# A written-out order of tasks and PSUM banks in place of a list scheduler, in a gated spectral and dense mix

## The chip, the cores and the metric

The kernel runs on one core of a Trainium2 chip. The metric is the device time of one execution in microseconds, as a median over runs. The engines are TensorE (PE, with its weight loads as PEld), VectorE (DVE), ScalarE (ACT), GpSimd (POOL) and SyncE (SP). Each runs its own instruction stream in order, and the streams meet at semaphores. SP, ACT and POOL also issue DMAs, which run on 16 engines that all queues share.

## The reference: what is computed

```python
x = A_x                                             # (1, 2048, 512) bf16
g = sigmoid((x * gate_w).sum(-1, keepdims=True))    # one gate a row
X = rfft2(x, axes=(-2, -1)) * (w_r + 1j * w_i)      # w: (2048, 257)
a = irfft2(X, s=(2048, 512))                        # spectral branch
h = x @ w1 + b1                                     # (2048, 512) @ (512, 1792)
b = (h * tanh(softplus(h))) @ w2                    # mish, (1792, 512)
return g * a + (1 - g) * b
```

There are two branches over the same 2048 x 512 input. The dense branch is two matrix products with a Mish between them. The spectral branch is a two-dimensional real Fourier transform, a product with a weight per frequency, and the way back; the kernel does the transforms as products with constant matrices. A gate per row mixes the two.

## The kernel before, in words

The program is a graph of 578 tasks, each with an engine, its reads and writes, and a few instructions. A task's name tells its stage:

- `ld_x`, `ld_w1`, `ld_w2`, `ld_W` and others are loads. x comes in pieces: x0 to x3 one row tile each, x4 and x6 two tiles (256 KB), x8 and x12 four tiles (512 KB). SP and ACT issue x, w1 and the constants at the start. POOL issues the two halves of w2 (`ld_w2_0`, `ld_w2_1`, 896 KB each) and the eight pieces of the spectral weight (`ld_W00` to `ld_W13`, 257 KB each), all behind the landing of `ld_sm`.
- `warm` and `tr` are the first TensorE work: 16 matmuls on zeros, and transposes of x (line 525), four for a row tile. `tr_small` transposes the bias. `evx` evicts them into xT. `table` (line 470) is a Mish of one element, ahead of which ScalarE loads its function table.
- Dense: `mm1_c_ft` (line 846) is four 128x512 matmuls for chunk c of 512 rows (0 to 3) and feature tile ft (0 to 13); `mish_c_ft` (line 853) evicts it on ScalarE with Mish into one of three buffers. `mm2_t_0` and `mm2_t_1` (line 870) are the two halves of the second product for row tile t, seven matmuls each; the first half reads `ld_w2_0`, the second `ld_w2_1`. Row tile 15 is cut by columns instead. `bev_t` evicts a row tile with the factor (1 - g), `sum_t` adds the spectral part, `out` stores it; tiles 14 and 15 use `fin_t` (line 882), which does both in one instruction.
- Spectral forward: `a10_t` and `a11_t` (line 563, four matmuls each) transform two row tiles along the row, `eg`, `e1p`, `e1m`, `e1f` evict and combine them, `s1_t` (line 594, 16 matmuls) is the first step along the columns, `e2_t` evicts it into Ybuf, and `r1w` stores it to a scratch tensor in DRAM in 16 pieces. When all 16 have landed `r1r0` to `r1r3` read it back in another layout into Abuf. `s2_vc` (line 735) is the second step, `wm` multiplies by the weights on VectorE, `wz` combines on GpSimd, `s2i_v` (line 766) starts the way back. `s2c`, `cvec`, `crv`, `rcc` and others handle one column apart; `wcols` on GpSimd and `rcw` on TensorE (lines 640 and 641) prepare its weights and need all eight `ld_W`.
- Spectral back: `e4`, `r2w`, `r2r` are a second trip through DRAM, into T2r; then for each of 16 row tiles `s1i` (line 795), `e5`, `a1i` (line 807), `gc`, `sap` and `sam` (line 818), `sbp` and `sbm` give the spectral part in `ga`.
- `gdot`, `gpow`, `gadd`, `gcol`, `omg` make the gates.

PSUM has eight banks. A task that starts a product names the banks it may have, and whoever gets a bank next waits for all readers of what stood there.

What sets the order of the work is `_Graph.schedule`, a list scheduler that runs when the program is built. It keeps a modelled time per engine, takes the ready tasks whose modelled start is within 0.03 us of the earliest, and picks the one with the highest priority (a table `PR` by stage, with a little random noise from a fixed seed), then the longest remaining path. It picks the engine for tasks that can run on several, and the bank that is free first. The result is one list of tasks per engine; semaphore waits are derived from it. `run_engine` then emits each list. At the end of SP's list stand the closing waits:

```python
for t in G.tasks:
    if t.isdma and t.sem is not out_sem and seen.get(t.sem.num, 0) < t.semval:
        eobj.wait_ge(t.sem, t.semval)
eobj.wait_ge(out_sem, 16 * n_out_dma[0])
```

They ask for every DMA that SP hasn't waited for already; there are 38 of these (the loads, ld_g1, ld_gd and the four r2r). In the program they stand two to an instruction.

Of the kernel before, what the change touches and what calls it, by code (L numbers as in the profile page):

```python
# [107 lines left out]
class _Ps:  # L108


    __slots__ = ("options", "bank", "sl", "nfree", "consumers", "done")

    def __init__(self, options):
        self.options = [o if isinstance(o, tuple) else (o,) for o in options]
        self.bank = None
        self.nfree = 0
        self.consumers = []
        self.done = 0.0
# [30 lines left out]
SCH = dict(eps=0.03, sync=0.05)  # L149
LAT = {"act": 0.11, "dve": 0.08, "pool": 0.05, "pe": 0.0, "sp": 0.0}  # L150


class _Graph:
# [49 lines left out]
    def schedule(self):  # L203
        tasks = self.tasks
        sync = SCH["sync"]
        eps = SCH["eps"]
        for t in tasks:
            for d in t.deps:
                d.succ.append(t)
        for t in reversed(tasks):  # L210
            m = 0.0
            for s_ in t.succ:
                m = max(m, s_.bl)
            t.bl = t.dur + t.lat + t.xfer + m
        nleft = {id(t): len(t.deps) for t in tasks}
        ready = [t for t in tasks if not t.deps]
        rng = np.random.RandomState(SEED)
        prio = {id(t): t.prio + OFFS.get(_kind(t.name), 0.0) + NOISE * rng.uniform(-1, 1) for t in tasks}
        free = {e: 0.0 for e in self.ENGS}
        order = {e: [] for e in self.ENGS}  # L220
        bank_free = [0.0] * 8
        bank_prev = [()] * 8
        port = 0.0
        dq = 0.0
        gen = {}
        left = len(tasks)
        while left:
            cand = []
            for t in ready:
                opts = t.opts or ((t.eng, t.dur, t.fn, t.lock),)  # L230
                bo = None
                for (oe, od, of, ol) in opts:
                    e_ = max(free[oe], port) if ol else free[oe]
                    for d in t.deps:
                        e_ = max(e_, d.start + d.dur if d.eng == oe == "pe" else d.done + (0.0 if d.eng == oe else sync))
                    if oe == "pe" and e_ < COLD:
                        od *= 2
                    if bo is None or e_ + od < bo[0] - 1e-9:
                        bo = (e_ + od, e_, oe, od, of, ol)
                est = bo[1]  # L240
                if t.alloc is not None:
                    got, used = [], set()
                    for p in t.alloc:
                        best = None
                        for o in p.options:
                            if any(bank_free[b] is None or b in used for b in o):
                                continue
                            f = max(bank_free[b] for b in o)
                            if best is None or f < best[0] - 1e-9:
                                best = (f, o)  # L250
                        if best is None:
                            break
                        est = max(est, best[0] + sync)
                        got.append(best[1])
                        used.update(best[1])
                    if len(got) < len(t.alloc):
                        continue
                    cand.append((est, t, bo, got))
                else:
                    cand.append((est, t, bo, None))  # L260
            if not cand:
                raise RuntimeError('no bank for ' + str([t.name for t in ready]))
            lo = min(c[0] for c in cand)
            near = [c for c in cand if c[0] <= lo + eps]
            first = {}
            for c in near:
                if c[1].isdma:
                    first[c[1].eng] = min(first.get(c[1].eng, c[1].idx), c[1].idx)
            pick = max((c for c in near if not c[1].isdma or first[c[1].eng] == c[1].idx),
                       key=lambda c: (prio[id(c[1])], c[1].bl, -c[1].idx))  # L270
            est, t, bo, banks = pick
            _, _, t.eng, t.dur, t.fn, lk = bo
            ready.remove(t)
            t.start = est
            free[t.eng] = est + t.dur
            if lk:
                port = est + t.dur
            if banks is not None:
                have = set(map(id, t.deps))
                for p, bk in zip(t.alloc, banks):  # L280
                    for b in bk:
                        for d in bank_prev[b]:
                            if id(d) not in have:
                                have.add(id(d))
                                t.deps.append(d)
                        bank_free[b] = None
                    p.bank = bk[0]
                    p.sl = slice(bk[0], bk[-1] + 1, max(1, bk[-1] - bk[0]))
                    p.options = [bk]
            if t.isdma:  # L290
                gen[t.eng] = max(est + t.dur, gen.get(t.eng, 0.0)) + 0.003 * t.nd
                xs = max(est + t.dur + 0.7, dq)
                dq = max(xs + t.xfer, gen[t.eng] + 0.3)
                t.done = dq + t.lat
            else:
                t.done = est + t.dur + t.lat + LAT[t.eng]
            for p in t.frees:
                p.nfree -= 1
                p.consumers.append(t)
                p.done = max(p.done, t.done)  # L300
                if p.nfree == 0:
                    for b in p.options[0]:
                        bank_free[b] = p.done
                        bank_prev[b] = tuple(p.consumers)
            order[t.eng].append(t)
            left -= 1
            for s_ in t.succ:
                nleft[id(s_)] -= 1
                if nleft[id(s_)] == 0:
                    ready.append(s_)  # L310
        self.order = order
        self.makespan = max(t.done for t in tasks)
        return order


NBF = 14
# [5 lines left out]
SEED = 272  # L322
NOISE = 0.02
OFFS = {}
# [4 lines left out]
COLD = 6.5  # L329
# [3 lines left out]
def _build(nc, A_x, A_w_r, A_w_i, B_x, B_w1, B_b1, B_w2, gate_w, out):  # L333
# [8 lines left out]
    with es:  # L342
# [566 lines left out]
        def run_engine(ename, eobj):  # L909
            seen = {}  # L910
            for t in order[ename]:
                need = {}
                for d in t.deps:
# [6 lines left out]
                    if val > need.get(sem_.num, (None, 0))[1]:  # L920
                        need[sem_.num] = (sem_, val)
                for key, (sem_, val) in need.items():
                    if seen.get(key, 0) < val:
                        seen[key] = val
                        eobj.wait_ge(sem_, val)
# [5 lines left out]
            if ename == "sp":  # L931
                for t in G.tasks:
# [69 lines left out]
```

## Time and profile before

| what | value |
|---|---|
| median of 3 runs | 136.58 us (136.18, 136.58, 137.93) |
| profiled execution, span from first to last instruction | 135.4 us |
| PE, DVE, ACT, POOL busy, share of the span | 94%, 66%, 53%, 42% |
| mean granted TensorE clock | 0.987 |
| moved by DMA | 21.09 MB, mean 156 GB/s |
| chain that ended last, largest shares | PE 87% (L870 36%, L846 34%), DMA 7% |

The profile gives the execution's span and not a time of its own; the median of the runs is 1.2 us above the span and the lowest 0.8. A line of the timeline or of the chain has the start and the duration in microseconds, then the engine, the line of the program, the operation and how often it stands there; brackets hold how long the engine was idle before it and what ended that. A row of waits has the total, how many, and the longest. A row of windows has the stretch, its length, the busy time of PE, PEld, DVE, ACT and POOL with the number of instructions, then the granted clock, the busy share of the DMA engines, and GB/s. A DMA row has the count, the size of one, and the median time from issue to landing.

### The profile page before, as it was taken

Reading aid. Unit: us, or ns where it says so; the run is one execution under the profiler, and the core shown is the slowest. Engines: PE = TensorE matmul, PEld = TensorE weight load, DVE = VectorE, ACT = ScalarE, POOL = GpSimd, SP = SyncE. Lnnn points to the kernel's source line nnn. Section 1 sums busy time; section 2 is a strip of 40 time slices with the busy share of each in tenths; the row PEclk is TensorE's granted clock in tenths of the full one; section 3 lists DMA queues with packets and bytes.
Section 4 is the critical chain, followed back from the end, with each engine's and each line's share of the span. In section 5 each row is a group of like instructions: output and inputs, shape, how many; then the busy total and the mean of one; then the engine's idle time right before and its main releaser. Section 6 shows DMA issues by size and latency. Waiting matters only on the chain.

```text
span 135.4 us, 2511 instructions
## 1 busy us (share of the span) xinstructions
PE 127.3 (94%) x947; PEld 65.5 (48%) x947; DVE 89.8 (66%) x163; ACT 71.8 (53%) x116; POOL 56.8 (42%) x87
## 2 busy tenths in 40 slices
PE   6739999999999999799999999999999999999991
PEld 4517666555445544234433333444656556546560
DVE  0437598997887961395979973300398997794941
ACT  0423468789888888460434678842664466434120
POOL 3000007900021935029999758000069498558100
PEclk9996899999999999999999999999999999999999
DMA  4899951999956644938013310559700212201212
GB/s 116 257 285 420 372 169 24 339 312 221 236 121 194 194 125 115 381 159 310 0 49 110 110 48 25 158 145 307 299 0 5 90 65 82 77 16 64 77 58 99
DMA packets 16888, 21.09 MB, mean 156 GB/s; under 512 B 1196, under 2 KB 13356, under 8 KB 16492
## 3 DMA queue, kind: packets, MB, share of 16 engines
q1 hardware_dynamic: 14736, 15.95, 35.7%
q0 software_dynamic: 864, 3.94, 11.1%
q10 hardware_dynamic: 1276, 1.05, 2.6%
q8 instruction: 7, 0.11, 0.4%
q14 instruction: 5, 0.04, 0.1%
HBM read 14.64 MB, written 6.29 MB: 155 GB/s over the span
## 4 chain that ended last, share of the span: by engine, by line
PE 87%; DMA 7%; SPq 2%; DVE 0%; issue 0%
PE ps L870 36%; PE ps L846 34%; DMA xo<-in_A_x_dram 4%; PE ps L563 3%; DMA Abuf<-scr 3%; PE ps L594 3%; PE ps L795 3%; PE ps L807 3%; SPq L420 2%; PE ps L525 2%; PE ps L735 2%; PE ps L766 2%; DVE xo L882 0%; PE ps L690 0%; PE ps L640 0%
## 5 line engine op out<-in xcount | busy, mean ns | idle before, releaser
L846 PE MATMUL ps<-xT,w_sb 128*128 128x512 bf16 x224 | 54.0, 386 | 0.0
L870 PE MATMUL ps<-w_sb,act 128*128 128x512 bf16 (+1 forms) x238 | 51.6, 367 | 0.0
L853 ACT ACTIVATE act<-ps,b1f 128x512 bf16<-128x512 f32 x56 | 38.5, 687 | 17.2 <-PE ps L846 17.0
L870 PEld LDWEIGHTS ps<-w_sb,act 128*128 128x128 bf16 x238 | 22.3, 98 | 22.4 <-issue 0.7
L846 PEld LDWEIGHTS ps<-xT,w_sb 128*128 128x128 bf16 x224 | 20.5, 99 | 25.0 <-issue 3.9
L455 POOL TENSOR_TENSOR Tg<-Qb 128x256 bf16<-128x256 f32 x28 | 20.4, 760 | 21.3 <-DVE Qb L818 21.3
L455 POOL TENSOR_TENSOR Zb<-Qb 128x510 bf16<-128x510 f32 x16 | 19.8, 1264 | 9.6 <-DVE Qb L455 9.6
L828 ACT ACTIVATE xo<-ps,omg 128x512 bf16<-128x512 f32 x14 | 9.6, 687 | 24.3 <-PE ps L870 24.3
L455 DVE TENSOR_TENSOR Qb<-ps,WT 128x1024 f32<-128x1024 f32 x16 | 18.6, 1218 | 3.7 <-PE ps L735 2.9
L818 DVE SCALAR_TENSOR_TENSOR Qb<-ps,gcol,Qb 128x256 f32<-128x256 f32 x32 | 13.5, 474 | 2.0 <-PE ps L807 1.9
L450 DVE CAST Ybuf<-ps 128x1024 bf16<-128x1024 f32 x8 | 9.8, 1225 | 6.7 <-PE ps L766 5.0
L450 DVE CAST Zb<-ps 128x512 bf16<-128x512 f32 x8 | 5.5, 688 | 12.6 <-PE ps L795 11.7
L612 DVE SCALAR_TENSOR_TENSOR Tg<-xo,Tg 128x512 bf16<-128x512 bf16 x16 | 11.1, 691 | 0.8 <-DVE Tg L612 0.5
L455 DVE TENSOR_TENSOR Abuf<-ps,Tg 128x512 bf16<-128x512 f32 x16 | 10.4, 685 | 1.5 <-ACT Tg L570 0.9
L812 ACT ACTIVATE Qb<-ps,gcol 128x256 f32<-128x256 f32 x16 | 7.0, 472 | 7.5 <-PE ps L807 7.5
L420 POOL DMA_DIRECT2D w_sb<-in_B_w_dram x2 | 2.2, 1080 | 19.3 <-DMA sm<-c_sm 19.3
L450 DVE COPY xT<-ps 128x1024 bf16<-128x1024 bf16 (+1 forms) x9 | 5.4, 628 | 7.2 <-PE ps L525 7.1
L451 ACT ACTIVATE Ybuf<-ps 128x1024 bf16<-128x1024 f32 x8 | 8.2, 1024 | 2.6 <-PE ps L766 1.5
L455 DVE TENSOR_TENSOR xo<-xo,Tg 128x512 bf16<-128x512 bf16 x14 | 8.5, 634 | 1.4 <-ACT xo L828 1.3
L525 PE MATMUL ps<-ident,xo 128*128 128x128 bf16 x64 | 4.7, 225 | 2.2 <-DMA xo<-in_A_x_dram 2.2
L563 PEld LDWEIGHTS ps<-FDs,Tg 128*128 128x128 bf16 x64 | 5.0, 105 | 2.4
L570 ACT ACTIVATE Tg<-ps 128x512 f32<-128x512 f32 x8 | 4.6, 590 | 2.8 <-PE ps L563 2.8
(68 smaller groups left out, 85.5 us busy)
## 6 DMA issues: line engine op xcount, KB each, us to landing
Abuf<-scr SPq DMA_DIRECT2D x8, 512.0 KB, 5.5
scr<-Ybuf SPq DMA_DIRECT2D x16, 128.0 KB, 2.2
scr<-Ybuf SPq DMA_DIRECT2D x4, 512.0 KB, 3.2
w_sb<-in_B_w_dram POOLq DMA_DIRECT2D x2, 896.0 KB, 7.0
out_dram<-xo SPq DMA_DIRECT2D x7, 256.0 KB, 2.0
WT<-in_A_w_r_dram POOLq DMA_DIRECT2D x4, 257.0 KB, 9.0
WT<-in_A_w_i_dram POOLq DMA_DIRECT2D x4, 257.0 KB, 11.7
xo<-in_A_x_dram SPq DMA_DIRECT2D x2, 512.0 KB, 7.8
```

The costliest lines, as they stand in the source:

```text
L450: fs = {"dve": ("dve", dve_dur(n, rate=rate), lambda e: e.tensor_copy(out=dst(), in_=src())), "act": ("act", act_dur(n), lambda e: e.activ ...
L451: "act": ("act", act_dur(n), lambda e: e.activation(dst(), src(), AF.Copy))}
L455: f = lambda e: e.tensor_tensor(out=o(), in0=i0(), in1=i1(), op=op)
L525: ins = e.transpose(psb[:, pt.bank, o:o + 128], xo[:, t0 + i, d0:d0 + 255:2], ident[:, :])
L563: ins = e.matmul(ps[:, pa.bank, 256 * i:256 * i + 256].rearrange("p (s m) -> p s m", s=4)[:, r:4 - r:3 - 2 * r, :], Tb[:, hb, 2 * r + half ...
L612: lambda e, t=t: e.scalar_tensor_tensor(out=junk, in0=xo[:, t, :], scalar=1.0, in1=gwb, op0=ALU.mult, op1=ALU.mult, accum_out=gdot[:, t:t ...
L812: lambda e, t=t, sl=sl, p5=p5: e.activation(gC[:, sl, :].rearrange("p (i n) -> p i n", i=2), ps[:, p5.bank, :].rearrange("p (i n) -> p i n ...
L818: lambda e, t=t, sl=sl, p5=p5, o=o, op=op: e.scalar_tensor_tensor(out=st1[:, sl, o::2, :], in0=ps[:, p5.bank, :].rearrange("p (i n) -> p i ...
L828: G.add_multi(f"bev_{t}", [("act", act_dur(512, True), lambda e: e.activation(xo[:, t, :], ps[:, pd.bank, :], AF.Copy, scale=omg[:, t:t + ...
L846: ins = e.matmul(ps[:, pd.bank, :], w1_sb[:, i, 128 * ft:128 * (ft + 1)], xT[:, i, 512 * c:512 * c + 512], start=(i == 0), stop=(i == 3))
L853: lambda e, ft=ft, pd=pd, hb=hb: e.activation(act[:, hb, ft, :].rearrange("p (t a b) -> p t a b", t=4, b=2), ps[:, pd.bank, :].rearrange(" ...
L870: ins = e.matmul(ps[:, pd.bank, cs_], act[:, hb, ft, 128 * tl:128 * (tl + 1)], w2_sb[:, ft, cs_], start=(ft == 0), stop=(ft == NFT - 1))
```

## The change

`schedule` no longer searches. A string `ORDER` of 1476 characters lists all 578 tasks: two characters in base 62 for a task, one letter for its engine where it has a choice, and one digit for each bank it gets. The function walks the string, gives each task its engine and bank, adds the readers of what stood in the bank to the task's dependencies, and checks that no task stands ahead of what it needs. The priorities' seed, noise and cost tables go. The tasks and their instructions are the same.

```diff
     def schedule(self):
         tasks = self.tasks
-        sync = SCH["sync"]
-        eps = SCH["eps"]
...
         order = {e: [] for e in self.ENGS}
...
+        held = [None] * 8
+        pos = 0
...
+        for _ in tasks:
+            t = tasks[digit(2)]
+            if t.opts:
+                t.eng, t.dur, t.fn = next(o[:3] for o in t.opts if o[0] == ENGINE[ORDER[pos]])
+                pos += 1
+            for p in t.alloc or ():
+                b0 = digit(1)
+                p.bank = b0
+                p.banks = range(b0, b0 + len(p.options[0]))
+                p.sl = slice(b0, b0 + len(p.options[0]))
+                for b in p.banks:
+                    if held[b] is not None:
+                        if held[b].nfree:
+                            raise RuntimeError("bank in use: " + t.name)
+                        t.deps += [d for d in held[b].consumers if d not in t.deps]
+                    held[b] = p
             for p in t.frees:
                 p.nfree -= 1
                 p.consumers.append(t)
-                p.done = max(p.done, t.done)
...
+            t.start = float(len(order[t.eng]))
             order[t.eng].append(t)
...
+ORDER = (
+    "040O0N2r00020730Q0P0108090S0R0A0B0C0D0T0E0U030F0G0V0W0H050I0X060J0v70Z0x00wv0z40b0Y0yv0K0L10v0a1120M0c121Gv6L6"
...
         def run_engine(ename, eobj):
             seen = {}
+            closed = []
             for t in order[ename]:
...
+                if ename == "sp" and t.sem is out_sem and not closed:
+                    closed.append(t)
+                    for d in G.tasks:
+                        if d.isdma and d.sem is not out_sem:
+                            need.setdefault(d.sem.num, (d.sem, d.semval))
...
             if ename == "sp":
-                for t in G.tasks:
-                    if t.isdma and t.sem is not out_sem and seen.get(t.sem.num, 0) < t.semval:
-                        eobj.wait_ge(t.sem, t.semval)
                 eobj.wait_ge(out_sem, 16 * n_out_dma[0])
```

Read as task names, the string says the following. TensorE up to the second column step (x..y for a run of tasks, warm-up left out):

```
before: tr1 tr0 tr2 tr_small mm1_0_0 tr4 tr6 a10_2 a10_0 a11_0 a11_2 mm1_0_1 mm1_0_2
        tr10 tr8 a11_6 mm1_0_3 a11_4 tr12 mm1_0_4 mm1_0_5 tr14 mm1_0_6 a10_6 mm1_0_7 a11_8
        a10_4 mm1_0_8 a11_10 mm1_0_9 a11_12 mm1_0_10..11 a10_10 mm1_0_12 a10_8 mm1_0_13
        a11_14 mm1_1_0..1 a10_14 mm1_1_2..3 a10_12 mm1_1_4..5 s1_4 mm1_1_6..8 s1_0
        mm1_1_9..10 s1_8 mm1_1_11..12 rcw mm1_1_13 s1_12 mm1_2_0..10 s2_01 s2_00
        mm1_2_11..13 mm2_2_0 s2c s2_10 s2_11 mm2_0_0 rcc mm2_0_1 ...
after:  tr0 tr1 tr2 tr_small mm1_0_0 mm1_0_1 tr4 mm1_0_2 a10_0 a11_0 mm1_0_3 tr6 tr8
        mm1_0_4 a11_2 a10_2 mm1_0_5 tr10 mm1_0_6 tr12 mm1_0_7..9 a10_4 a11_4 mm1_0_10 tr14
        a11_6 mm1_0_11..13 a10_6 mm1_1_0..3 a10_8 mm1_1_4 s1_0 a10_10 mm1_1_5 a11_8
        mm1_1_6..7 a11_10 mm1_1_8 s1_4 mm1_1_9 mm2_0_0 rcw s1_8 a10_12 mm2_0_1 a10_14
        a11_12 mm2_1_0 a11_14 mm1_1_10..11 s1_12 mm1_1_12..13 mm1_2_0..5 mm2_1_1 mm2_2_0
        s2_00 s2_01 mm1_2_6 mm2_2_1 mm1_2_7 s2c mm1_2_8 s2_10 s2_11 mm2_3_0 ...
```

TensorE's last tasks were `mm2_15_0 a1i_15 mm2_13_0 mm2_14_1 mm2_13_1 mm2_15_1` and become `mm2_13_0 a1i_13 a1i_15 mm2_13_1 mm2_14_0 mm2_14_1 mm2_15_0 mm2_15_1`. On the other engines:

- ACT's first tasks were x1, x3, w1_0_1, b1, w1_2_1, x6, w1_4_1, table; table now stands ahead of x6 and w1_4_1.
- POOL's loads were w2_0, w2_1, W00, W01, W02, W03, W10, W11, W12, W13; they become W11, w2_0, W00, W10, W01, W13, W12, W02, W03, w2_1.
- SP's loads stay as they were; the r1w stores go in the order of their tiles, a piece and its twin together, where before tiles 6 and 4 went first.
- VectorE ends with `sbm_14 sbm_15 sbp_15 fin_14_1 fin_15_0 sum_12 sum_13 fin_15_1` (before: `... fin_14_1 fin_15_0 sum_13 fin_15_1`, with sum_12 earlier).
- 21 tasks change engine: nine e5 (six to ScalarE, three to VectorE), five e4 (three to ScalarE, two to VectorE), four e1f (three to ScalarE, one to VectorE), bev_3 and bev_7 to VectorE, sbp_14 to GpSimd.
- Most products get other banks; s2_10 gets the banks of s2_01.

The closing waits move ahead of SP's first store, out1, and only the wait for all stores is left at the end.

133 lines of the change are left out of this document (27 added, 106 removed).

## The prediction

> **What bounds the kernel now.** I read the page first: its shares, then its slices.
>
> ```profile
> span 135.4 us, 2511 instructions
> PE 127.3 (94%) x947; PEld 65.5 (48%) x947; DVE 89.8 (66%) x163; ACT 71.8 (53%) x116; POOL 56.8 (42%) x87
> PEclk9996899999999999999999999999999999999999
> ```
>
> TensorE works for 94% of the span, so an order can win only where TensorE idles, where its clock is low, or behind its last matmul. The PEclk line has one dip, in slices 4 and 5. Next come TensorE's own waits and its timeline, which place the idle time.
>
> ```profile
> PE ps L525 <- DMA xo<-in_A_x_dram: 2.2, 1, 2.2
> PE ps L534 <- DMA braw<-in_B_b_dram: 1.0, 1, 1.0
> PE ps L735 <- DMA Abuf<-scr: 0.7, 1, 0.7
> ```
>
> ```profile
> 6.62 1.03 PE L846 MATMUL ps<-xT,w_sb 128*128 128x512 bf16 x4
> 9.85 1.07 PE L525 MATMUL ps<-ident,xo 128*128 128x128 bf16 x16 [2.20 <-DMA xo<-in_A_x_dram]
> 15.04 1.06 PE L525 MATMUL ps<-ident,xo 128*128 128x128 bf16 x16
> 55.87 0.63 PE L735 MATMUL ps<-Abuf,sm 64*32 64x512 bf16 x16 [0.68 <-DMA Abuf<-scr]
> 126.21 6.22 PE L870 MATMUL ps<-w_sb,act 128*128 128x512 bf16 x35
> ```
>
> After mm1_0_0 TensorE stands 2.20 us, since tr4 is next in its order and ld_x4 has not landed. It stands 0.68 us once more, before s2. From 55.87 us to its end at 132.4 no DMA holds it. The windows show what the first hole does to the clock (the number behind the busy times):
>
> ```profile
> 10.00:11.00 1.00, 1.00 (x21) 1.00 (x20) 0.49 (x1) 0.00 (x0) 0.00 (x0) 1.00 1.07 422
> 11.00:12.00 1.00, 1.00 (x14) 1.00 (x12) 0.79 (x2) 0.82 (x2) 0.00 (x0) 0.53 1.04 426
> 13.00:14.00 1.00, 1.00 (x4) 0.42 (x3) 1.00 (x3) 0.00 (x0) 0.00 (x0) 0.50 1.01 396
> 14.00:15.00 1.00, 1.00 (x5) 0.37 (x4) 0.30 (x1) 0.69 (x1) 0.00 (x0) 0.77 1.07 365
> ```
>
> From 11.0 to about 14.4 us the granted clock is half, so some 1.7 us of work is lost beside the 2.2 us of idle time.
>
> The prices come from the chain that ended last (start, duration, what):
>
> ```profile
> 3.90 5.90 DMA xo<-in_A_x_dram
> 17.40 0.45 PE ps L525 x8
> 21.97 0.45 PE ps L563 x8
> 30.66 1.73 PE ps L846 x8
> 44.60 0.99 PE ps L594 x16
> 45.59 6.11 PE ps L846 x28
> 51.70 4.13 DMA Abuf<-scr
> 90.50 4.53 PE ps L870 x21
> ```
>
> So at full clock: an mm1 block 0.865 us (half of 1.73), an mm2 half 1.51 (a third of 4.53), an s1 task 0.99, eight matmuls of 128 columns 0.45 (tr4, or two tasks of a1).
>
> **The change, part by part.** No matmul is added or removed, so what TensorE doesn't do in one place it does in another. I therefore compare what has been done when s2 starts, behind which both orders run without a load to wait for.
>
> *Start.* The new TensorE order runs mm1_0_1 before tr4, then mm1_0_2, the a1 pair of tile 0, mm1_0_3, tr6, tr8. On ScalarE the table stands ahead of ld_x6 and ld_w1_4_1.
>
> ```profile
> 5.08 1.28 ACT L470 ACT_TABLE_LOAD   x1 [5.08 <-issue]
> 5.38 0.63 SPq L420 DMA_DIRECT2D xo<-in_A_x_dram  x1
> xo<-in_A_x_dram SPq DMA_DIRECT2D x2, 512.0 KB, 7.8
> DMA to landing us min/median/max: 2.7/4.2/8.4
> ```
>
> mm1_0_1 ends at 6.62 + 2 x 0.865 = 8.35. tr4 then needs x4, at 9.80 today. The table (1.28 us and its 0.2 us activation) delays x6 by 1.5 us and leaves the DMA engines to x4: between 8.35 and 9.80, and I take 8.7. From there 0.45 + 0.865 + 0.45 + 0.865 + 0.45 = 3.08 us lead to tr8 at 11.8 (11.4 to 12.9 by the bounds). tr8 needs ld_x8, which SP issues at 5.38. The two 512 KB loads take 7.8 in the middle and 8.4 at most, so the other takes 7.2: x8 lands at 12.6. So tr8 ends near 13.05, whichever way x4 goes. Four mm1 blocks are done there. The first hole shrinks to about 0.35 and one of 0.8 stands at tr8; no stretch of 3.4 us has more than 1.2 us idle, against 2.2 now, so I let the clock stay full. (The 1.0 us of L534, ahead of all this, cost no clock.)
>
> The Trainium skill, "TensorE: Matmul & The Clock Gate" (Why this matters for your kernels), warns of idle gaps above some 3 us. Here 2.2 us came before the drop, so the measurement decides; by that rule the dip would not hang on this hole, and would stay (second rival).
>
> *POOL's loads.* The order becomes W11, w2_0, seven more W, then w2_1 last; all are still behind ld_sm.
>
> ```profile
> 21.10 2.16 POOL L420 DMA_DIRECT2D w_sb<-in_B_w_dram  x2 [19.28 <-DMA sm<-c_sm]
> 25.26 1.95 POOL L420 DMA_DIRECT2D WT<-in_A_w_i_dram  x4
> 39.92 0.19 POOL L631 COPY wrv<-WT 128x2 bf16<-128x2 bf16 x1 [12.71 <-DMA WT<-in_A_w_i_dram]
> ```
>
> The ten loads land by 39.8 today, and TensorE doesn't feel it, since mm2 comes after 59 us. The new order puts mm2_0_0 and mm2_0_1 ahead of s1_12, and mm2_0_1 needs w2_1. From tr8 TensorE reaches it after 20 mm1 (17.30), 24 transposes (1.35), 11 a1 tasks (2.47), three s1 (2.97), one mm2 half (1.51): 25.6 us. Summed this way, the stretch of now from tr10 at 15.04 to the hole at 55.19 (36 mm1, 32 transposes, 12 a1, 4 s1) gives 39.6 us against 40.15, so I add 1.4%: 26.0, arrival 39.0. The last load: 39.8, less 0.55 since the first issue is now a W (1.95 / 4 = 0.49 us) and not a w2 (1.08), plus what the r1w stores take, which now start near 31 us instead of 36.4:
>
> ```profile
> scr<-Ybuf SPq DMA_DIRECT2D x3, 128.0 KB, 3.9
> scr<-Ybuf SPq DMA_DIRECT2D x16, 128.0 KB, 2.2
> 36.00:37.00 1.00, 1.00 (x6) 0.41 (x5) 1.00 (x2) 1.00 (x2) 0.00 (x0) 1.00 1.09 263
> 37.00:38.00 1.00, 1.00 (x7) 0.33 (x7) 0.50 (x3) 0.71 (x2) 0.00 (x0) 1.00 0.96 193
> 40.00:42.00 2.00, 2.00 (x21) 1.01 (x20) 1.05 (x4) 1.52 (x4) 1.11 (x4) 1.00 0.69 198
> ```
>
> (The first row is of the stretch 36 to 40 us.) With the loads running, three stores took 3.9 us in the middle, where all 16 have a median of 2.2; with the engines to themselves a store of 131 KB at 198 GB/s and a share of 0.69 costs 0.46 us. Up to eight can meet the loads: 0 to 3.7 us. They waited more than they were served, so I take 0.3. w2_1 lands at 39.55: a new hole of 0.55 us. rcw, which needs the eight W, has w2_1's time as its margin.
>
> The Trainium skill, "DMA: Bandwidth & Descriptors" (Queues, rings and completion order), has each DMA engine take turns between queues by whole packets of some 9 to 17 descriptors. Then early stores would take turns from the loads, which speaks against this change; that 3.9 us store waited longer than turns would ask (third rival).
>
> *s2.* Behind mm2_0_1 come 10 mm1, 4 mm2 halves, 3 a1, one s1: 16.4, with 1.4% 16.6 us, so TensorE reaches s2 at 39.6 + 16.6 = 56.2. The other way there: s1_12 ends 10.1 us of TensorE work earlier (8 mm1, 2 halves, 1.4%), at 46.1. Today s1_12 ends at 45.59 and the first r1r lands at 55.83, 10.24 later; so 56.35, which wins. That is 0.5 later than 55.87, but five mm2 halves are done (7.55) against five mm1 blocks more today (4.33): 3.2 us ahead. Gain at s2: **2.7 us**.
>
> *Behind s2.* s2_10 takes the bank of s2_01 and waits for the four products of VectorE:
>
> ```profile
> 56.35 4.62 DVE L455 TENSOR_TENSOR Qb<-ps,WT 128x1024 f32<-128x1024 f32 x4 [2.92 <-PE ps L735]
> ```
>
> They end 0.48 + 4.62 = 5.1 us after s2's start. TensorE is there after 0.63 + 3 x 0.865 + 1.51 + about 0.2 (s2c) = 4.9: loss **0.2 us**. The 21 tasks that change engine (e5 mostly to ScalarE, two bev to VectorE) cost what they free, under the cover of TensorE; ScalarE and VectorE are at 53 and 66%. Without that cover an eviction costs about 0.7 us; I take nothing, bounds -0.5 and 1.0 over all. At the end fin_15_0, sum_12, sum_13 stand before fin_15_1 on VectorE, some 1.35 to 1.9 us under a last half of 1.5: nothing to 0.4.
>
> *Closing waits.*
>
> ```profile
> L934 SPq EVENT_SEMAPHORE  x18: 28/28/28, 133.4 to 134.8; - x18
> L935 SPq EVENT_SEMAPHORE  x1: 28/28/28, 134.9 to 134.9; - x1
> L420 SPq DMA_DIRECT2D out_dram<-xo x10: 332/332/414, 104.8 to 133.0; - x10
> DMA to landing us min/median/max: 1.6/2.0/2.0
> ```
>
> The last store goes out at 133.0 and lands at 134.6, but SP reaches its final wait only at 134.9, through 18 instructions of two waits each. Ahead of out1 they cost the same 1.5 us, while SP waits for the first sum anyway; behind SP are then only the stores, the first at 104.8. Everything they ask for has landed when T2r is read. Gain **0.3 us**; without the cover, out1 is 1.5 us late and nobody waits for it.
>
> Sum: -2.7 + 0.2 - 0.3 = -2.8 of 135.4, so a span of 132.6. The median of the runs shown, 136.58, is 1.2 above the span; I keep that distance: **133.8 us**, 2.0% less. Two per cent is about what a measurement of this kernel can tell from no change: the three runs lie 1.3% apart.
>
> **The rivals.**
>
> 1. The holes only move: x8, w2_1 and r1r are DMAs that the order hardly speeds, and each can stand where x4 stood. For it: two new waits above. Against it: the mm2 halves fill time in which only mm1 was ready. If the r1r chain also grows by 2 us, 0.8 is left: 135.8.
> 2. The clock still halves, through x4 at 9.80 and x8's wait in one stretch: 1.7 us lost, of which the 0.55 in front of w2_1 is absorbed: 134.9.
> 3. Slower: w2_1 lands late. Place: mm2_0_1 holds s1_12, so the whole spectral chain. Each us costs one. The gain of 2.8 is gone when w2_1 lands at 42.35; eight stores served ahead of it (3.7 us, not 0.3) make 42.95, and 137.2. Against it: the stores of now that waited.
>
> **How the numbers follow.** The forecast has 0.64, with a range of its own from 133.0 (w2_1 no bound, 0.55, and evictions slightly better) to 134.7 (evictions 1.0 worse); its middle stands on the line of 2%. Rival 1 has 0.14, rival 2 0.10, rival 3 0.12. The range from 132.9 to 136.4 leaves out rival 3 and some of the edges. Faster by over 2% (under 133.85): 0.7 of the forecast, 0.45. Slower by over 2% (above 139.3) needs rival 3 and more: 0.06. Within: 0.49.
>
> **What would show it.** PEclk without a dip; TensorE's wait for xo split in two, together near 1.1 us; a wait of L870 for w_sb near 39 us of about 0.5; s2 near 56.3; SP's waits of L934 gone from the end and its last wait right behind the landing. A wait of L641 for wrv, a w_sb wait above 2 us, or a dip in PEclk makes it wrong on the slow side; a w_sb wait of nothing and s2 before 55.8 on the fast side.

## The result, and the profile after

| | before | after |
|---|---|---|
| median of 20 runs each, side by side | 137.72 us (135.49 to 140.5) | 135.69 us (133.73 to 138.07) |
| profiled execution: span, mean granted clock | 135.4 us, 0.987 | 133.5 us, 1.000 |

The ratio is 0.9861 with a 95% interval of 0.9818 to 0.9905: 1.4% faster, by more than the interval and by less than 2%. A ratio leaves out runs more than 1.5% above their kernel's fastest, so it can differ a little from the ratio of the medians (0.9853). The runs of before have a median 1.1 us above the 136.58 that was shown; the three runs behind that figure lay low. In every run on record whose span is known the time is 1.7 to 1.8 us above the span. So the profiled execution of before, with its span of 135.4, took about 137.1 us (an estimate from that distance), 0.5 more than the median of 136.58 that was set beside it.

The page of the kernel after, its span, busy shares and clock by slices:

```profile
span 133.5 us, 2492 instructions
PE 124.5 (93%) x931; PEld 65.1 (49%) x947; DVE 87.7 (66%) x158; ACT 72.2 (54%) x120; POOL 57.3 (43%) x88
PEclk9999999999999999999999999999999999999999
```

The dip in slices 4 and 5 is gone. Next TensorE's waits (total, how many, longest), and its timeline at the places that the prediction named:

```profile
PE ps L581 <- POOL wrv L573: 2.3, 1, 2.3
PE ps L466 <- DMA xo<-in_A_x_dram: 1.5, 2, 1.2
PE ps L475 <- DMA braw<-in_B_b_dram: 0.3, 1, 0.3
```

```profile
5.03 0.61 PE L466 MATMUL ps<-ident,xo 128*128 128x128 bf16 x8 [0.30 <-DMA xo<-in_A_x_dram]
6.60 1.89 PE L787 MATMUL ps<-xT,w_sb 128*128 128x512 bf16 x8
9.67 0.62 PE L466 MATMUL ps<-ident,xo 128*128 128x128 bf16 x8 [1.19 <-DMA xo<-in_A_x_dram]
12.30 1.06 PE L466 MATMUL ps<-ident,xo 128*128 128x128 bf16 x16
39.98 0.20 PE L581 MATMUL ps<-wrv,flip 128*128 128x64 bf16 x1 [2.29 <-POOL wrv L573]
41.35 1.67 PE L811 MATMUL ps<-w_sb,act 128*128 128x512 bf16 x7
57.89 0.62 PE L676 MATMUL ps<-Abuf,sm 64*32 64x512 bf16 x16
```

(The lines of the program have moved: mm1 is now L787, mm2 L811, the transposes L466, rcw L581 and L582, s1 L535, s2 L676, a DMA L361.) The hole of 2.20 us in front of tr4 has become 1.19 us. The other wait for xo, 0.30 us at 5.03, belongs to the first transposes; at tr6 and tr8 (12.30) there is no hole, since ld_x8 landed at 12.47 and TensorE came to tr8 only at 12.75. The 0.68 us in front of s2 are gone. In their place stands a wait that before did not have: 2.29 us in front of rcw at 39.98 us, for the last piece of the spectral weight. s2 starts at 57.89 us against 55.87 before, with 3.2 us more of TensorE's work done. The store that closes the program:

```profile
L361 SPq DMA_DIRECT2D out_dram<-xo x10: 332/332/349, 105.8 to 131.5; - x10
SPq L881 <- DMA out_dram<-xo: 1.2, 1, 1.2
```

The last store goes out at 131.5 and lands at 133.08 us; SP waits for it and for nothing behind it. From that landing to the end of the span there are 0.41 us, where before had 0.84.

### The profile page after: what moved, and what is told of

It reads as the page before. It is cut to its first block, busy times and chain, and to the rows that moved or that the text cites. A ratio compares the mean times of both kernels' runs of the same rounds, so it can differ in the third digit from the quotient of the medians.

```text
span 133.5 us, 2492 instructions
## 1 busy us (share of the span) xinstructions
PE 124.5 (93%) x931; PEld 65.1 (49%) x947; DVE 87.7 (66%) x158; ACT 72.2 (54%) x120; POOL 57.3 (43%) x88
## 4 chain that ended last, share of the span: by engine, by line
PE 57%; DMA 22%; SPq 8%; DVE 5%; POOL 4%; issue 2%; POOLq 0%
PE ps L811 31%; PE ps L787 15%; DMA WT<-in_A_w_r_dram 11%; SPq L361 8%; DMA sm<-c_sm 6%; DVE Qb L396 3%; DMA Abuf<-scr 3%; PE ps L736 3%; POOL WT L361 3%; PE ps L748 3%; DMA scr<-Ybuf 2%; PE ps L707 2%; PE ps L676 2%; PE ps L535 1%; DVE Ybuf L391 1%
## 5 line engine op out<-in xcount | busy, mean ns | idle before, releaser
L787 PE MATMUL ps<-xT,w_sb 128*128 128x512 bf16 x215 | 51.8, 379 | 0.6 <-issue 0.2
L794 ACT ACTIVATE act<-ps,b1f 128x512 bf16<-128x512 f32 x56 | 37.7, 687 | 26.9 <-PE ps L787 26.7
L811 PE MATMUL ps<-w_sb,act 128*128 128x512 bf16 (+1 forms) x231 | 51.2, 366 | 0.4 <-issue 0.2
L811 PEld LDWEIGHTS ps<-w_sb,act 128*128 128x128 bf16 x238 | 22.2, 98 | 23.1 <-issue 2.0
L787 PEld LDWEIGHTS ps<-xT,w_sb 128*128 128x128 bf16 x224 | 20.8, 98 | 22.3 <-ACT act L794 0.4
L396 POOL TENSOR_TENSOR Tg<-Qb 128x256 bf16<-128x256 f32 x29 | 22.3, 795 | 18.1 <-DVE Qb L759 18.1
L396 DVE TENSOR_TENSOR Qb<-ps,WT 128x1024 f32<-128x1024 f32 x16 | 18.7, 1218 | 4.5 <-PE ps L676 4.0
L391 DVE CAST Ybuf<-ps 128x1024 bf16<-128x1024 f32 x7 | 8.6, 1224 | 9.5 <-PE ps L707 5.1
L769 ACT ACTIVATE xo<-ps,omg 128x512 bf16<-128x512 f32 x12 | 8.2, 690 | 8.1 <-PE ps L811 8.1
L392 ACT ACTIVATE Ybuf<-ps 128x1024 bf16<-128x1024 f32 x9 | 9.1, 1023 | 6.1 <-PE ps L535 5.3
L361 POOL DMA_DIRECT2D WT<-in_A_w_i_dram x4 | 2.3, 572 | 18.2 <-DMA sm<-c_sm 18.2
L396 DVE TENSOR_TENSOR xo<-xo,Tg 128x512 bf16<-128x512 bf16 x14 | 7.8, 579 | 0.2 <-POOL Tg L396 0.2
L558 POOL TENSOR_TENSOR gcol<-omg,gdot 128x16 f32<-128x16 f32 x1 | 2.9, 2943 | 10.3 <-DVE Tg L553 10.3
L392 ACT ACTIVATE Zb<-ps 128x512 bf16<-128x512 f32 x11 | 6.5, 602 | 1.5 <-PE ps L736 1.5
L466 PE MATMUL ps<-ident,xo 128*128 128x128 bf16 x64 | 4.8, 222 | 1.5 <-DMA xo<-in_A_x_dram 1.5
```

Source lines behind the costliest of these rows:

```text
L361: t = G.add(name, queue, 1.0 if queue == "pool" else issue, lambda e: e.dma_start(dst, src), reads=reads, writes=writes, lat=tail, deps=de ...
L391: fs = {"dve": ("dve", dve_dur(n, rate=rate), lambda e: e.tensor_copy(out=dst(), in_=src())), "act": ("act", act_dur(n), lambda e: e.activ ...
L392: "act": ("act", act_dur(n), lambda e: e.activation(dst(), src(), AF.Copy))}
L396: f = lambda e: e.tensor_tensor(out=o(), in0=i0(), in1=i1(), op=op)
L466: ins = e.transpose(psb[:, pt.bank, o:o + 128], xo[:, t0 + i, d0:d0 + 255:2], ident[:, :])
L769: G.add_multi(f"bev_{t}", [("act", act_dur(512, True), lambda e: e.activation(xo[:, t, :], ps[:, pd.bank, :], AF.Copy, scale=omg[:, t:t + ...
```

## The experiments

Three theories were open after this. **Clock**: the main gain is the half clock behind the first hole, which the new order avoids in some runs only. **Order**: at equal clock the mm2 halves ahead of s1_12 give most. **Loads**: the new stall at rcw takes back what the order gives. Each run has a mean granted clock; one stretch of 3.41 us at half clock makes 0.987 of a span of 134 us, two make 0.975, so a run without a profile also tells how many such stretches it had.

**b_close: the order of before, with the closing waits moved.**

```diff
-    closing waits behind SP's last store
+    closing waits in front of out1
     (order and banks as before)
```

> The order and the banks of the kernel before, with the closing waits ahead of out1. Theory: the waits are all that stood between the landing of the last store and the end, so the span ends 0.4 us behind that landing instead of 0.84 us; TensorE's last matmul stays near 132.4 us, the first store near 104.8 us, and the span is 135.0 us (ratio 0.997). Rival: out1 goes out late and the stores behind it queue up; then the last store lands later and the gain is gone.

Measured: 138.12 us in 10 runs beside 138.42 of before in 19 on the same chip. The medians say 0.3 us less and the ratio, 1.0077 (1.0006 to 1.0147), says more, so the times show no gain. The profiled span is 135.66 us and not the 135.0 expected, since TensorE waited 1.26 us in front of s2. In the profile, from the last landing at 135.24 to the end at 135.66 there are 0.42 us, the same as after, against 0.84. So the closing waits give 0.42 us by the profiles; the times are too scattered to add to this.

None of these 10 runs had the full clock: six had one stretch at half, four two. The windows of the profile of b_close show where it begins (busy times of the engines, then the granted clock):

```profile
9.00:10.00 1.00, 0.00 (x0) 0.00 (x0) 0.00 (x0) 0.00 (x0) 0.00 (x0) 0.93 1.04 368
10.00:11.00 1.00, 0.81 (x8) 0.81 (x9) 0.00 (x0) 0.00 (x0) 0.00 (x0) 0.50 1.12 436
```

**b_start: b_close, with mm1_0_1 ahead of tr4, as after has it.**

```diff
-    PE: ... mm1_0_0 tr4 tr6 a10_2 ...
+    PE: ... mm1_0_0 mm1_0_1 tr4 tr6 a10_2 ...
```

> b_close with one task moved: mm1_0_1 stands right behind mm1_0_0, ahead of tr4. Theory: what the new order gains early comes from this one place. TensorE's wait for x falls from 2.2 to 1.35 us, the clock stays full in most runs, and with 0.86 us of idle time filled and up to 1.7 us of half clock saved the span is 132.4 to 133.0 us (ratio 0.979 to 0.985). Rival: the gain comes from the dense work moved ahead of s2; then at most the 0.86 us shows, and the clock still halves between 11 and 14 us.

Measured: 136.05 us in 10 runs, ratio 0.9912 (0.9814 to 1.001), 2.1 us under b_close on the same chip. Six runs had the full clock (median 135.44), four one stretch at half (137.39). One block of 0.87 us moved ahead of the hole gives, by the medians, as much as the whole change, and most of it by the clock: 0.4 stretches a run where b_close has 1.4. It does not do so in every run: in the profile x4 landed at 10.80 and the hole was as long as ever. The six spans at full clock, 133.0 to 134.5 us, are longer than the 132.4 to 133.0 expected.

```profile
6.59 1.89 PE L787 MATMUL ps<-xT,w_sb 128*128 128x512 bf16 x8
10.85 1.30 PE L466 MATMUL ps<-ident,xo 128*128 128x128 bf16 x16 [2.37 <-DMA xo<-in_A_x_dram]
```

**a_warm: the kernel after, with nine dummy matmuls in front of tr4.**

```diff
-    PE: ... mm1_0_1 tr4 ...
+    PE: ... mm1_0_1 warm16 ... warm24 tr4 ...
```

> The changed kernel with nine more warm-up matmuls of 256 columns behind mm1_0_1, so that TensorE works while it waits for x4; they compute nothing that is used. Theory: the runs of the changed kernel with a mean clock of 0.987 lost one stretch of half clock to the idle time of 1.2 us in front of tr4; here every run has a clock of 0.999 or more, the profiled span stays at 133.5 us, and the ratio falls from 0.986 to about 0.978. Rival: the stretch of half clock belongs to the 2.3 us in front of rcw; then clocks of 0.987 go on in about half of the runs, here and not in a_fill.

Measured: 134.39 us in 4 runs, ratio 0.9825 (0.968 to 0.997). Three had the full clock (134.26 in the middle), one did not (136.51), so the expectation of every run at full clock was missed. The hole in front of tr4 was still 0.72 us in the profile, and whether the dummies raised the share above one half four runs can't tell.

**after_again: the kernel after unchanged, on the chip of a_useful and a_best.**

> The changed kernel as it is, once more and on one chip with the three below. Theory: about half of its runs keep a mean clock of 1.000 with spans of 132.0 to 134.4 us, the others have 0.987 and lose some 2 us; the kernel before has 0.987 or 0.975 in nearly every run. So the medians are 2.0 to 2.5 us apart (ratio 0.982 to 0.986). Rival: the share of full clock was chance; then it is far from half here.

Measured: 135.66 us in 10 runs, ratio 0.9853 (0.9782 to 0.9925). Five runs had the full clock, four one stretch at half, one two, as expected. Its profile has a hole of 2.31 us in front of tr4, and the full clock all the same:

```profile
10.91 0.62 PE L466 MATMUL ps<-ident,xo 128*128 128x128 bf16 x8 [2.31 <-DMA xo<-in_A_x_dram]
39.56 0.20 PE L581 MATMUL ps<-wrv,flip 128*128 128x64 bf16 x1 [0.42 <-POOL wrv L573]
```

So neither the hole nor the wait at rcw has one size. x4 landed at 9.63 us in one execution and at 10.86 in the other; when the first hole is long, TensorE comes late to rcw and waits less there (2.29 and 0.42 us; the last W also landed 0.5 us sooner in the second). That is why the spans are nearly the same, 133.5 and 133.7.

**a_useful: real work in front of tr4 instead of dummies.**

```diff
-    PE: ... mm1_0_1 tr4 mm1_0_2 a10_0 a11_0 mm1_0_3 tr6 tr8 mm1_0_4 ...
+    PE: ... mm1_0_1 a10_0 a11_0 mm1_0_2 mm1_0_3 tr4 tr6 mm1_0_4 tr8 ...
     (eg_0, e1p_0, e1m_0 earlier on their engines, another bank for a11_0)
```

> The changed kernel with the work that is ready put into the wait for x4: behind mm1_0_1 come a10_0, a11_0, mm1_0_2 and mm1_0_3, then tr4, tr6, mm1_0_4, tr8 (ScalarE and VectorE follow). Theory: TensorE's wait in front of tr4 goes from 1.2 to 2.0 us down to 0.3 or nothing, no stretch of 3.4 us is idle enough, and at least 9 of 10 runs have a clock of 0.998 or more; median 1.2 us below after_again. Rival: the clock halves for another reason; then as many runs as in after_again have 0.987.

Measured: 134.53 us in 4 runs (134.51 to 134.90), ratio 0.9824 (0.9722 to 0.9925), all at full clock. The wait has moved to the weights and is 1.4 us; the one at rcw is 1.5 in this profile:

```profile
PE ps L581 <- POOL wrv L573: 1.5, 1, 1.5
PE ps L787 <- DMA w_sb<-in_B_w_dram: 1.4, 1, 1.4
```

**b_warm: the order of before, closing waits moved, with twenty dummy matmuls in the hole.**

```diff
-    PE: ... mm1_0_0 tr4 tr6 ...
+    PE: ... mm1_0_0 warm16 ... warm35 tr4 tr6 ...
```

> The order of before, with the closing waits in front of the first store, and twenty dummy matmuls of 256 columns (they compute nothing that is used) behind mm1_0_0, about 2.1 us at full clock, so that TensorE does not stand still until x4 lands. Theory (the hole halves the clock): the granted clock is then full in nearly all runs, tr4 still starts when x4 has landed (9.7 to 10.8 us), and the median falls from the 138.1 us of b_close by 1.1 to 1.3 half-clock windows of 1.7 us, so by 1.9 to 2.2, to 136.0 (135.6 to 136.6). The new order is then left with 0.3 to 0.8 us at equal clock beside it. Rival (the clock is set by something other than the hole): most runs keep 0.987 or 0.975 and the median stays within 0.6 of 138.1.

Measured: 135.24 us in 4 runs (135.03 to 136.37), ratio 0.9788 (0.9719 to 0.9856), all at full clock. Before on the same chip has 138.37 in 7 runs, none at full clock. This is the old order with the closing waits moved and nothing useful added, and it is as fast as the kernel after. Against b_close it is 2.9 us less, more than the 1.9 to 2.2 expected; b_close's own 1.4 stretches at 1.7 us make 2.4, and its wait of 1.3 us in front of s2 was absent here. The two ran on different chips, so the 0.5 left is not settled. The rival, that something other than the hole sets the clock, fell.

The profile of this run came with a late x4:

```profile
PEclk9999999999999999999999999999999999999999
7.73 2.35 PE L416 MATMUL ps<-act 128*128 128x256 bf16 x20
11.96 1.07 PE L466 MATMUL ps<-ident,xo 128*128 128x128 bf16 x16 [1.88 <-DMA xo<-in_A_x_dram]
```

Again a hole, of 1.88 us, without half clock. At equal clock the kernel after (134.76 in the middle of its 15 runs) stands 0.5 us under this one, inside the 0.3 to 0.8 expected, but not on one chip. The section on the hardware puts these holes side by side.

**a_loads: the kernel after, with POOL's loads in the order of before.**

```diff
-    POOL: W11 w2_0 W00 W10 W01 W13 W12 W02 W03 w2_1
+    POOL: w2_0 w2_1 W00 W01 W02 W03 W10 W11 W12 W13
```

> The changed kernel with the loads of GpSimd in the order of the kernel before (both w2, then the eight W). Theory: the r1w stores that now start near 31 us, not the order of the loads, stretch the last load; the time from the first issue to the last landing stays above 19 us, W13 lands near 39 us or later, rcw waits 2 us or more, and mm2_0_1 waits for nothing. Rival: mixing w2 and W is what stretches it; then the last load lands 18.7 us behind the first issue, as in the kernel before.

Measured: 135.53 us in one run, span 133.8 at 0.987 (its hole at tr4 was 2.29 us, and the clock halved from 11.94). No wait at rcw at all, against an expected 2 us or more:

```profile
10.66 0.62 PE L466 MATMUL ps<-ident,xo 128*128 128x128 bf16 x8 [2.29 <-DMA xo<-in_A_x_dram]
12.00:13.00 1.00, 1.00 (x10) 0.98 (x9) 0.01 (x1) 0.69 (x1) 0.00 (x0) 0.50 1.02 418
```

The expectation fell, though not for the loads alone: behind a long hole and half clock TensorE came to rcw at 40.39, where in after it was there at 37.69 (39.98 less 2.29). The last W of this run landed at 38.17, that of after at 38.90, so with TensorE on time rcw would have waited here too; on that wait the run is inconclusive. What it does show is the last landing of all: in the old order the ten loads are done 18.1 us after the first is issued, in the new one after 21.2 (w2_1 at 41.28) or, in after_again, 19.7.

**a_late_r1w: the kernel after, its first r1w store held until w2_1 has landed.**

```diff
-    dma("r1w0a", ...)
+    dma("r1w0a", ..., deps=[ld_w2_1])
```

> The kernel after with its first r1w store waiting for w2_1, so no store shares the DMA engines with the ten loads. If the early stores stretch the loads: w2_1 lands at 38.5 to 39.6 instead of 41.3, W03 before 38. If they wait and take nothing until the loads drain, and the order of the loads alone stretches them: w2_1 still lands at 40.5 to 41.3 and TensorE still waits 0.4 to 2.3 us at rcw. The stores themselves then land some 3 us after their issue instead of 9 to 10, and s2 comes at 57.9 to 58.9.

Measured: 135.57 us in one run, span 133.8 at full clock. This shows what the early stores take from the loads. First the DMA issues of the stretch 26 to 47 us of the kernel after, then of a_late_r1w (count, size, median us to landing):

```profile
scr<-Ybuf SPq DMA_DIRECT2D x12, 128.0 KB, 5.2
w_sb<-in_B_w_dram POOLq DMA_DIRECT2D x1, 896.0 KB, 16.0
```

```profile
scr<-Ybuf SPq DMA_DIRECT2D x10, 128.0 KB, 2.2
w_sb<-in_B_w_dram POOLq DMA_DIRECT2D x1, 896.0 KB, 14.7
39.40 0.20 PE L581 MATMUL ps<-wrv,flip 128*128 128x64 bf16 x1 [1.36 <-POOL wrv L573]
```

w2_1 lands at 40.55 us, 19.9 us after the first issue. That is no shorter than in the other profiles with the new load order and early stores, 19.5 to 20.0 in six of them; the 21.2 of the profile of after is the odd one. The wait at rcw stays and s2 starts at 58.15, as expected for stores that take nothing. So the stores take too little to see. The last landing comes later with the new order of the loads: 19.5 to 21.2 us after the first issue in eight profiles, with the old one 18.4 to 18.7 in before and b_close, 18.1 in a_loads, 19.2 in b_start and 19.4 in b_warm. The means, 20.0 and 18.8, are 1.2 us apart; a single pair of profiles can't show it.

**a_fill: the kernel after, with other work between mm2_0_0 and s1_12.**

```diff
-    PE: mm1_1_9 mm2_0_0 rcw s1_8 a10_12 mm2_0_1 a10_14 a11_12 mm2_1_0 a11_14 mm1_1_10 mm1_1_11 s1_12 mm1_1_12 mm1_1_13
+    PE: mm1_1_9 mm2_0_0 s1_8 a10_12 mm1_1_10 mm1_1_11 rcw a10_14 a11_12 mm1_1_12 a11_14 mm2_0_1 mm1_1_13 s1_12 mm2_1_0
     (ScalarE's mish, eg, e1f and e2 of the stretch follow; three tasks get other banks)
```

> The changed kernel with TensorE's work around rcw moved: s1_8, a10_12, mm1_1_10 and mm1_1_11 go ahead of rcw, mm1_1_12 and a11_14 ahead of mm2_0_1, and mm2_1_0 behind s1_12 (ScalarE's evictions follow). Theory: the 2.3 us in front of rcw are lost on the spectral chain, because s1_8 and s1_12 stand behind rcw, which waits for the last of the eight W; here rcw waits for nothing, s1_12 ends near 45.5 instead of 47.9 us, s2 starts near 55.6 instead of 57.9, and the span is 131.3 us. Rival: the trip through DRAM or VectorE takes over, s1_12 or s2 waits, and the span stays at 133.0 to 133.5 us.

Measured: 133.91 us in 4 runs, ratio 0.9784 (0.9622 to 0.9945). In TensorE's waits L581 is gone, and s1_12 and s2 start earlier by 1.6 and 1.7 us:

```profile
41.22 0.19 PE L581 MATMUL ps<-wrv,flip 128*128 128x64 bf16 x1
45.28 1.06 PE L535 MATMUL ps<-Abuf,m1g 64*128 64x256 bf16 x16
```

Its runs at full clock (133.55 in the middle of three) stand 1.2 us under those of after (134.76 in the middle of 15). a_best, below, has the same edit on top of a_useful and stands 1.6 us under it on the same chip. That is what rcw and mm2_0_1 cost where they stand, ahead of the landing of the loads. The span is 131.8 us against the expected 131.3, and s2 comes at 56.21 against 55.6; the rival, that another wait takes the gain, fell. One of the four runs had a stretch at half clock (136.43).

**a_best: a_useful and a_fill together; a_best_warm: the same with eight dummies in its last hole.**

```diff
     a_best = both edits
-    PE: ... a10_0 a11_0 mm1_0_2 ...
+    PE: ... a10_0 warm16 ... warm23 a11_0 mm1_0_2 ...    (a_best_warm)
```

> a_useful and a_fill together: the early wait filled, and the work around rcw moved. Theory: the two losses are apart, so both gains add: clock 0.998 or more in at least 9 of 10 runs, rcw without a wait, a span of 130.8 to 131.6 us and a median 2 us below after_again (ratio to the kernel before 0.965 to 0.970). Rival: the loads of w2 and W bound s1_8 and mm2_0_1 as soon as TensorE comes there earlier; then a_best stays within 0.5 us of a_useful.

> a_best with eight dummy matmuls of 256 columns (0.87 us, nothing of them is used) behind a10_0, in the 0.87 us in which mm1_0_2 waits for its weights. Theory: that hole cost one of a_best's four runs its clock (135.96 against 132.5 to 132.9), so now all runs have the full clock, with a median of 132.6 to 132.9 and none above 133.6. Rival: a hole of 0.87 us is too short to matter and something else took the clock in that run: one run in four still loses about 3 us.

Measured: a_best 132.89 us in 4 runs, ratio 0.9696 (0.9594 to 0.9799), three at full clock and one at 0.986 (135.96), short of the nine in ten expected. a_best_warm 132.97 us in 4 runs (132.55 to 133.15), ratio 0.9604 (0.9535 to 0.9672), all at full clock. Four runs against four don't prove that the dummies saved the clock, but the run of 136 us is not there. The page and TensorE's waits of a_best_warm:

```profile
PE 126.8 (97%) x955; PEld 66.5 (51%) x955; DVE 87.9 (67%) x158; ACT 71.9 (55%) x120; POOL 57.2 (44%) x88
PE ps L416 <- DVE act L409: 1.2, 1, 1.2
PE ps L475 <- DMA braw<-in_B_b_dram: 0.5, 1, 0.5
```

No DMA holds TensorE after 6.6 us. Both beat the kernel before and the kernel after.

## Why the prediction was right or wrong

The forecast was 133.8 us; the median is 135.69, inside the wide range of 132.9 to 136.4 and outside the forecast's own of 133.0 to 134.7. 1.1 of the 1.9 us is the level of before (136.58 from three runs, 137.72 from twenty). Of the change itself, 2.8 us were forecast and 2.0 measured. Three steps failed. The hole in front of POOL's loads was put at 0.55 us, at mm2_0_1, and measured 2.29, at rcw: the largest error in the sum. The clock was taken to go from one stretch at half to none, and it went from 1.2 a run to 0.57. And the table was to let x4 land 1.1 us sooner, which it did by 0.2. The place of the gain, the reason for the first dip, the work ahead of s2 and the closing waits were right. The profiled spans show the terms:

| term | forecast | measured in the spans |
|---|---|---|
| TensorE would reach mm2_0_1, without a wait at rcw | 39.0 | 39.06 (41.35 less 2.29) |
| hole for POOL's loads | 0.55 | 2.29 (0.42 in after_again) |
| mm2_0_1 to s2 | 16.6 | 16.54 |
| gain at s2 | 2.7 | 1.2 (3.2 of work less 2.02) |
| s2 to TensorE's end, beside the work done earlier | -0.2 | +0.25 |
| closing waits | 0.3 | 0.42 |
| sum | 2.8 | 1.9 (135.4 to 133.5) |

**The start.** The step "the table ... leaves the DMA engines to x4 ... I take 8.7" failed. ScalarE's timeline of after, beside the queue of its DMA issues (ACTq):

```profile
3.85 1.28 ACT L411 ACT_TABLE_LOAD   x1 [3.85 <-issue]
3.91 0.56 ACTq L361 DMA_DIRECT2D xo<-in_A_x_dram  x1
```

The table load runs on the engine while ld_x6 goes out, 0.06 us later than before and not 1.5. So x4 landed hardly earlier: 9.63 us here, 9.80 before, and up to 10.86 for the same kernel. There is one hole of 1.19 us at tr4 and none at tr8, instead of 0.35 and 0.8. x8 landed at 12.47 (forecast 12.6), but TensorE came to tr8 only at 12.75, the forecast 3.08 us behind tr4's start at 9.67. So tr8 ends at 13.20 us, close to the forecast 13.05, by luck: the one hole is as long as the two that were expected, and x8 decides nothing.

**The clock.** "I let the clock stay full" holds for the profiled run and for half of the runs. Over all runs on record with their clock:

| | runs | full | one stretch at half | two |
|---|---|---|---|---|
| before | 39 | 4 (136.1 us) | 23 (138.2) | 12 (139.4) |
| after, after_again | 30 | 15 (134.8) | 13 (136.2) | 2 (138.2) |

Before loses 47 stretches in 39 runs, 1.2 each; after 17 in 30, 0.57 each. The term was 1.7 us, one stretch before and none after; it is 0.64 stretches, about 1.1 us. This is the second rival in half of the runs, though through the hole at x4 alone. That one profile stood for all executions of a kernel is the error beneath it. It also spoils "I keep that distance": the 1.2 us set the median of three low runs against the span of an execution that took longer, where each run by itself lies 1.7 above its span. The profiled run of after took 135.24 us, 1.74 above its span; the median of all runs lies 0.45 above that run. At equal clock the change is worth 1.3 us (136.1 to 134.8 for the runs at full clock, four of before); with 0.42 of it from the closing waits, the order alone gives about 0.9, or 0.5 by b_warm, which has the closing waits and the full clock, on another chip.

The Trainium skill, "TensorE: Matmul & The Clock Gate" (HAM oscillation — how this bites in real kernels), has idle gaps above some 3.4 us as those that matter. The trace disagrees: a gap of 2.2 us is enough, and b_warm, which fills much of it, keeps the full clock in four runs of four.

**POOL's loads.** "w2_1 lands at 39.55: a new hole of 0.55" is the term that failed; that the loads would make a new hole near there was right. The chain that ended last, in after:

```profile
24.79 14.12 DMA WT<-in_A_w_r_dram
41.52 1.51 PE ps L811 x7
46.94 0.99 PE ps L535 x16
58.38 4.63 DVE Qb L396 x4
63.05 0.62 PE ps L676 x16
```

w2_1 landed at 41.28, 1.73 us later than forecast and 2.2 behind TensorE's arrival at 39.06. The step "rcw ... has w2_1's time as its margin" placed the wait wrongly: TensorE is at rcw by 37.69, and the last W, W03, landed at 38.90, only 2.4 us ahead of w2_1; with GpSimd's copies behind it rcw could start at 39.98. The new order of the loads does not delay the W: the last lands 16.6 to 18.9 us after the first issue in eight profiles, with the old order 18.1 to 19.4 in five. It is rcw that moved, from 43.52 us in before to 37.69. The wait for wrv that was to make the forecast wrong on the slow side came, and mm2_0_1 behind it found w2_1 just landed. The price of the stores in that sum, 0.3 us, held as far as the runs tell (a_late_r1w). What was left out is that the last landing comes later with the new order of the loads, by 1.2 us in the mean of the profiles and by 2.6 in this one (21.2 against 18.7); I had only moved the last landing of before by 0.55 us for a first issue of half the length. Why the order does this is not shown. The third rival had the right stretch and the wrong cause, and it came to 1.7 us of its 3.4.

**s2.** Two paths were weighed and the later taken, the r1r chain at 56.35. s1_12 ended at 47.93 us instead of 46.1, and r1r landed at 57.36, 9.4 behind it and not 10.24. TensorE itself reached s2 at 57.89 and did not wait, so the other path won, by the forecast 16.6 us from mm2_0_1. In after_again the chain was last by 0.4 us. a_fill shows the forecast state: without the stall s2 starts at 56.21, just behind r1r's landing at 56.16 (forecast 56.35), and the span is 131.8 (forecast 132.6).

**Behind s2.** The four products of VectorE (58.38 + 4.63) do hold s2_10, as worked out: it starts at 63.05, 0.43 us behind the matmul ahead of it where 0.22 is usual, so TensorE lost the 0.2 us forecast. (Before had s2_10 in the bank of s2_01 too, but ran s2_01 first there; after runs s2_00 first.) The task changes cost nothing that the spans show; the stretch gained 0.25 us where 0.2 were to be lost, inside the bounds given.

**Rivals.** Rival 1, holes that only move, describes the load end best, with x4 in part and W03 in place of r1r; 135.8 was its time, and it had 0.14. That this stands next to the measured 135.69 is luck: it was a gain of 0.8 us from a level 1.1 too low, and the gain measured is 2.0.

## What to carry to other kernels

Where TensorE waits at the start, ask for each hole not only what it costs but whether it can halve the clock behind it: here shortening one such hole (b_start by one block moved, b_warm with dummy matmuls) was worth 2 us or more, as much as a new order of all 578 tasks. An order written out in full has no slack where a load lands late, so keep work that needs no DMA behind each such load (that edit gained 1.2 us in a_fill and 1.6 in a_best). One profiled execution of one kernel gives the size of a wait only for that execution; landings here moved by 1 to 2 us between runs, and terms that hang on one want a range or a chance.

## What the runs showed of the hardware

**A window of 3.41 us decides the clock, and it runs on its own time.** In before the clock goes full at 4.23 us, half at 11.06 and full at 14.47: two steps of 3.41 us, then one. In each of the four profiles with a stretch at half (before, b_close, b_start, a_loads) it lasts 3.41 us. Counting TensorE's idle time inside the window just ahead of a change gives:

| profile | window (us) | hole | idle in it | clock behind it |
|---|---|---|---|---|
| b_start | 8.11 to 11.52 | 2.37 | 2.37 | half |
| before | 7.65 to 11.06 | 2.20 | 2.2 | half |
| a_loads | 8.53 to 11.94 | 2.29 | 2.13 | half |
| b_close | 6.45 to 9.87 | 2.23 | 1.99 | half |
| b_warm | 9.61 to 13.02 | 1.88 | 1.88 | full |
| a_useful | 7.19 to 10.60 | 1.37 | 1.34 | full |
| after | 7.66 to 11.07 | 1.19 | 1.24 | full |

The edges are the events of the granted clock, taken forward in steps of 3.41 us. (The idle time is the window less the busy time of its matmuls; it holds small gaps beside the hole.) All seven agree with one limit between 1.88 and 1.99 us of idle time in a window. A hole of 2.31 us (after_again) that two windows share leaves both under it; the edges of that run are not in its trace, so this is argued. The limit also fits the shares of runs: with mm1_0_1 in front the hole was over 1.9 us in three of six such profiles (x4 landed at 9.63, 9.76, 9.96, 10.61, 10.80 and 10.86, and the last three are these); with the order of before the hole was over 1.9 us in both profiles without dummies. Why some runs have two such stretches is not settled. The limit holds for the way down. Ahead of its first event the clock is half, though the mean clock of a run counts that time as full: eight transposes near 5 us take 1.06 us in b_close, whose event comes at 6.45, and 0.61 in after, past its event at 4.25. And the way up asked for more: the window from 0.36 to 3.77 us of a_useful, with 0.88 us idle, left the clock at half until the next edge, 7.19. The Trainium skill, "TensorE: Matmul & The Clock Gate" (What's actually happening), gives a free-running window of 3413 ns, with which these edges agree.

**Stores waited behind loads until these had nearly drained.** In after the first eight r1w stores were issued from 31.5 us on; the four issued before 36 us took 9.3 us in the middle, where all 16 of before have 2.2. The stretch 31 to 36 us of the kernel after, its queues (packets, MB, share of 16 engines) and its DMA issues:

```profile
q0 software_dynamic: 210, 1.03, 102.4%
scr<-Ybuf SPq DMA_DIRECT2D x4, 128.0 KB, 9.3
```

q0 is the queue of POOL's loads. Beside it the view lists one packet of another kind for this stretch and none of q1, the queue that carries SP's transfers, so no packet of a store ran. From 37 to 38 us q1 has its first 18 packets beside 82 of q0; from 38 to 40 it has 1002 beside 56. By the Trainium skill, "DMA: Bandwidth & Descriptors" (Queues, rings and completion order), each DMA engine takes turns between its queues by packets; this trace disagrees for these 5 us.
